# Chunks in pairs on TensorE in an RWKV-5 attention with a SoLU feed-forward block

## The chip, the cores and the metric

The kernel runs on one core of one Trainium2 chip. The metric is the device time of one execution in microseconds (us), lower is better; where several runs of the same kernel stand together, their median is used.

## What is computed

Two blocks follow one another. The first is the RWKV-5 recurrence with batch 4, 8 heads, 768 steps and head size 48; the second takes its result, 3072 tokens of 384 values, through a feed-forward block of width 1024 with a softmax gate and a normalisation.

```
for t in range(S):
    cur = einsum('bhd,bhe->bhde', u * k_t, v_t)
    y[:, :, t] = einsum('bhd,bhde->bhe', r_t, state + cur)
    state = w * state + einsum('bhd,bhe->bhde', k_t, v_t)
x = y.transpose(0, 2, 1, 3).reshape(B * S, H * D)
h = x @ w_in
solu = h * softmax(h)
ln = (solu - mean(solu)) / sqrt(var(solu) + 1e-6) * g_ln
out = ln @ w_out
```

Inputs and results are float32. The weights `w_in`, `w_out` and `g_ln` come as 64-bit floats or as words of that layout, and the kernel converts them itself.

## The kernel before, in words

The kernel is `direct_path`. It assumes that the decays `w` and the weights lie in sane ranges, computes everything on that assumption, and at the end forms one flag, `bad`; if it is set, a slow path (`general_path`, L19) does the work over. With these inputs the flag isn't set.

**Chunks.** The sequence of each batch is cut into 6 chunks of 128 steps. With 4 batches these are N = 24 units (L458), ordered so that the four batches of one chunk follow one another. All work is done per unit, and a unit's state is needed again only four units later.

**What a unit needs.** `load` (L465) fetches k, r and v. `decay_k` and `decay_r` (L671, L678) multiply k and r by powers of the decay on GpSimd; `weigh` (L685) forms r times k times u there, and `sum_own` (L690) sums it per head on VectorE. `diagonal` (L694) writes these sums into the diagonal of the score tile AT, eight ScalarE instructions. k and r are needed turned (channels on the partitions). Up to unit 8, `turn_r` and `turn_k` (L706, L713) do it with TensorE transposes into PSUM and an evacuation. From unit 9 (`FIRST`) on, `halve_rk` (L853) splits the 32-bit words into 16-bit halves on ScalarE (k) and VectorE (r), a transposing DMA on SP's queue turns them (`turn`, L831), and `join_rk` (L863) puts them together again on VectorE. `scores` (L726) multiplies turned k by turned r, 16 matmuls in tiles of 64 by 64, into the PSUM tile `pss` of two banks, and copies what lies above the diagonal into AT with one masked copy (L735). `finish` (L749) computes y, first the product with the state, 12 matmuls in four column tiles of 32, then AT times v, 16 matmuls, and copies it to `xT` on ScalarE (L772). Then it forms k times v for the state (`kv_ps`, L778), adds it to the state on VectorE (L784) and multiplies by the decay on GpSimd (L785).

**The feed-forward part.** `ffn_in` (L790) multiplies xT by w_in: 6 matmuls of 512 columns into two PSUM banks (`h_ps`), and an exponential on ScalarE with its sum (L798). `unit` (L801) makes solu on VectorE (L805, L807) and then centres and squares it on ScalarE (L809, L810). `deviation` (L813) forms the scale on GpSimd. `halve_ln`, the transposing DMA and `join_ln` (L842, L848) turn solu like r and k. `ffn_out` (L867) multiplies by w_out, 8 matmuls of 384 columns, scales the result on ScalarE (L879) and stores it. A float32 matmul shows as two records in the trace, so 6 matmuls are x12.

**Order.** The schedule is written by hand: the order of the calls in the loop at L887 is the order of the instructions on each engine, and each engine works its queue in that order. At step i, the loop does scores of unit i+1, finish of i, `ffn_in` and `unit` of j = i-2 (LA = 2) and `ffn_out` of l = i-7 (LO = 5 more). From i = 7 on, one step is on TensorE: h, o, scores, y, kv. Until i = 6 there is no `ffn_out` and the weights are converted in between.

**Buffers.** [...] `psA` holds `pss` (2 banks), `psH` the h tile (2 banks), and `psM` rotates four banks among everything else (turned r and k, tables, y, kv, o). In SBUF, `halves` and the raw weight words share a ring of six (L505, L825), `kp` has 4 buffers, `e` 2, `lnT` 2.

**Checks.** `check_range` (L636) fetches the decays once more as a row at step 10 and compares them, on one partition. From step 12 on, `load_weights` fetches the 14 weight pieces (6 of w_in with 512 columns, 8 of w_out with 384) once more, one a step, and `check_words` (L555) takes their absolute sum on ScalarE and their minimum on VectorE. `check_sums` (L646) puts everything together at the end.

Of the kernel before, what the change touches and what calls it, by code (L numbers as in the profile page):

```python
# [399 lines left out]
def direct_path(  # L400
# [50 lines left out]
    psM = ctx.enter_context(tc.tile_pool(name="psM", bufs=4, space=PSUM))  # L451
# [27 lines left out]
    wrow = const.tile([1, dm], F32, name="wrow")  # L479
# [8 lines left out]
    pss = psA.tile([128, 2, HP, T], F32, name="at")  # L488
    nc.vector.memset(pss, 0.0)
# [13 lines left out]
    def load_weights(j):  # L503
        dst, src, _ = pieces[j]
        raws[j] = wpool.tile([128, dst.shape[1], 2], U32, tag="raw", name="raw", bufs=6)  # L505
        nc.sync.dma_start(out=raws[j].rearrange("p n o -> p (n o)"), in_=src)
# [48 lines left out]
    def check_words(j):  # L555
        raw = raws.pop(j)
        mag = wpool.tile([128, raw.shape[1]], F32, tag="mag", name="mag", bufs=2)
        nc.scalar.activation(out=mag, in_=raw[:, :, 1].bitcast(F32), func=ACT.Abs,
                             accum_out=total[:, j : j + 1])
        nc.vector.tensor_reduce(out=least[:, j : j + 1], in_=mag, axis=AX.X, op=ALU.min)  # L560
# [26 lines left out]
    for St in states:  # L587
# [12 lines left out]
                            op0=ALU.max, op1=ALU.min)  # L600
    for j in range(8):
        if j < 7:
            nc.vector.tensor_mul(pw[:, 0, j + 1], pw[:, 0, j], pw[:, 0, j])
            nc.vector.reciprocal(out=pw[:, 1, j], in_=pw[:, 0, j])
        if j == 0:
            nc.vector.tensor_copy(out=fore[:, :, T - 1 : T], in_=pw[:, 1, 0].unsqueeze(2))
        else:
            n = 1 << (j - 1)
            nc.vector.tensor_mul(tab[:, :, :, T - 2 * n : T - n], tab[:, :, :, T - n : T],
                                 pw[:, :, j - 1].unsqueeze(3).to_broadcast([128, 2, HP, n]))  # L610
# [6 lines left out]
    def turn_table(table, out):  # L617
        ps = psM.tile([128, HP, 128], F32, tag="m", name="kd_ps")
        for a in range(HP):
            nc.tensor.transpose(ps[:, a, :], table[:, a, :], ident)  # L620
        nc.scalar.copy(out=out, in_=ps)  # L621
# [11 lines left out]
    all_ok = const.tile([1, 1], F32, name="all_ok")  # L633
    bad = flag.tile([1, 1], mybir.dt.int32, name="bad")

    def check_range():  # L636
        nc.sync.dma_start(out=wrow, in_=w.rearrange("h d -> (h d)").partition_broadcast(1))

        ok = small.tile([1, dm], F32, tag="ok", name="ok", bufs=1)
        ok2 = small.tile([1, dm], F32, tag="ok2", name="ok2", bufs=1)  # L640
        nc.vector.tensor_single_scalar(out=ok, in_=wrow, scalar=LOW, op=ALU.is_ge)
        nc.vector.tensor_single_scalar(out=ok2, in_=wrow, scalar=HIGH, op=ALU.is_le)
        nc.vector.tensor_mul(ok, ok, ok2)
        nc.vector.tensor_reduce(out=all_ok, in_=ok, axis=AX.X, op=ALU.min)

    def check_sums():  # L646

        L = len(pieces)
        good = small.tile([128, 2, N + L], F32, name="good", bufs=1)
        low = small.tile([128, 1], F32, name="low", bufs=1)  # L650
        nc.vector.tensor_single_scalar(out=good[:, 0, :N], in_=sums, scalar=1.0 / MOST,
                                       op=ALU.is_ge)
        nc.vector.tensor_single_scalar(out=good[:, 1, :N], in_=sums, scalar=MOST, op=ALU.is_le)
        nc.vector.tensor_single_scalar(out=good[:, 0, N:], in_=least, scalar=FLOOR, op=ALU.is_ge)
        nc.vector.tensor_single_scalar(out=good[:, 1, N:], in_=total, scalar=CEIL, op=ALU.is_le)
        nc.vector.tensor_reduce(out=low, in_=good, axis=AX.XY, op=ALU.min)
        n_ps = psM.tile([1, 1], F32, tag="m", name="n_ps")
        nc.tensor.matmul(n_ps, low, ones, start=True, stop=True)
        nc.vector.tensor_scalar(out=bad, in0=n_ps, scalar1=all_ok, scalar2=127.5,
                                op0=ALU.mult, op1=ALU.is_lt)  # L660
# [10 lines left out]
    def decay_k(i):  # L671
        X = live.setdefault(i, {})
        X["kp"] = apool.tile([128, H, P], F32, name="kp", bufs=4)
        nc.gpsimd.tensor_mul(X["kp"].rearrange("p h d -> p (h d)"),  # L674
                             kpads[i % NLD].rearrange("p h d -> p (h d)"),
                             kdec.rearrange("p a d -> p (a d)"))
# [29 lines left out]
    def turn_r(i):  # L706
        rT = factors(i)["rT"]
        ps = psM.tile([128, HP, T], F32, tag="m", name="tr_ps")
        for a in range(HP):
            nc.tensor.transpose(ps[:, a, :], pair(rpads[i % NLD], a), ident)  # L710
        nc.vector.tensor_mul(rT, ps, fore)

    def turn_k(i):  # L713
        X = live[i]
        ps = psM.tile([128, HP, T], F32, tag="m", name="tk_ps")

        for a in range(HP):
            nc.tensor.transpose(ps[:, a, :], pair(X["kp"] if i > 0 else kpads[0], a), ident)  # L718
        if i > 0:
            nc.scalar.copy(out=X["kT"], in_=ps)  # L720
        else:
            nc.vector.tensor_mul(X["kT"], ps, back)
# [3 lines left out]
    def scores(i):  # L726
        X = live[i]
        A4 = X["AT"].rearrange("p (a q) t -> p q a t", q=2)
        for a in range(HP):
            for c in range(2):  # L730
                for q in range(2):
                    rows = slice(q * P, q * P + D)
                    nc.tensor.matmul(pss[ts(c, P), q, a, c * P :], X["kT"][rows, a, ts(c, P)],  # L733
                                     X["rT"][rows, a, c * P :], start=True, stop=True)
        nc.vector.copy_predicated(A4, later.unsqueeze(1).to_broadcast([128, 2, HP, T]), pss)  # L735
# [13 lines left out]
    def finish(i):  # L749
# [19 lines left out]
        for n, (m, h, at) in enumerate(inner):  # L769
            into(m, vf[:, at : at + 32], AT[:, h, :], last[m] == n)  # L770
        X["xT"] = fpool.tile([128, KD, 128], F32, name="xT", bufs=LA + 1)
        nc.scalar.copy(out=X["xT"], in_=y_ps)  # L772
        if c < C - 1:
            kv_ps = psM.tile([128, HP, D], F32, tag="m", name="kv_ps")
            for a in range(HP):
                for g in range(4):
                    h = 2 * a + g // 2
                    nc.tensor.matmul(kv_ps[ts(g, 32), a], X["kp"][:, h, ts(g % 2, 32)],  # L778
                                     vt[:, h, 0:D], start=True, stop=True)
            for q in range(2):  # L780
                wT = pw[ts(q, P), 0, 7].unsqueeze(2).to_broadcast([P, HP, D])
                S = St[ts(q, P), :, q]
                if c > 0:
                    nc.vector.tensor_add(S, kv_ps[ts(q, P)], S)  # L784
                    nc.gpsimd.tensor_mul(S, S, wT)  # L785
                else:
                    nc.vector.tensor_mul(S, kv_ps[ts(q, P)], wT)


    def ffn_in(i):  # L790
# [6 lines left out]
        e = X["e"] = fpool.tile([128, dff], F32, name="e")  # L797
# [89 lines left out]
    for i in range(-2, N + LA + LO):  # L887
        j, l = i - LA, i - LA - LO
        early = l < 0
        if i == -1:  # L890
            nc.sync.dma_start(out=g_sb, in_=moe_g_ln.rearrange("(c p) -> p c", p=128))
        if 0 <= i and i + 5 < N:
            load(i + 5, "kr")
        if 0 <= i and i + 3 < N:
            load(i + 3, "v")
        early_h = l <= 0
        if early_h and i >= LA:
            ffn_in(j)
# [4 lines left out]
        if i == -2:  # L903
            turn_r(0)
            turn_k(0)
            turn_table(back, kdec)
# [8 lines left out]
        if -2 < i and i + 2 < N:  # L915
            if i + 2 < FIRST:
                turn_r(i + 2)
            elif not early_h:
                join_rk(i + 2)
            if early_h and i >= LA:  # L920
                unit(j)
            if early_h and i + 2 >= FIRST:
                join_rk(i + 2)
            if i < 0 or i >= LA:
                sum_own(i + 2)
            if i + 2 < FIRST:
                turn_k(i + 2)
# [5 lines left out]
        if i + 3 < N and i != 1:  # L933
# [10 lines left out]
        if 1 <= i and i + 3 < N:  # L944
            weigh(i + 3, nc.gpsimd)
        if 0 <= j - 1 < N:
            deviation(j - 1)
        if i == 10:
            check_range()
        if 12 <= i < 12 + len(pieces):  # L950
            load_weights(i - 12)
        if 13 <= i < 13 + len(pieces):
            check_words(i - 13)
        if 0 <= l + 2 < N:
            halve_ln(l + 2)
        if 0 <= l + 1 < N:
            join_ln(l + 1)
        if i + 3 < N:
            halve_rk(i + 3)
        if not early:  # L960
            if j < N and not early_h:
                ffn_in(j)
            if i + 2 < N:
                diagonal(i + 2)
            if j < N and not early_h:
                unit(j)
            if l == N - 1:
                check_sums()
            ffn_out(l)
        if 0 <= i + 1 < N:  # L970
            scores(i + 1)
        if i < 0:
            diagonal(i + 2)
        if 0 <= i < N:
            finish(i)
        if i == 1:
            turn_table(fore, rdec)
            sum_own(3)
        if early and 0 <= i:
# [3 lines left out]
        if i >= LA:  # L983
            for p in before:
                convert_d(p)
            for p in now:
                convert_b(p)
    return bad
# [42 lines left out]
```

## Time and profile before

| | us |
|---|---|
| median of 3 runs | 354.89 |
| the three runs | 355.28, 354.89, 354.89 |
| the profiled execution, its own time | 355.35 |
| its span from the first to the last instruction | 353.5 |
| TensorE matmul busy | 338.0 |
| ScalarE busy | 242.1 |
| VectorE busy | 210.8 |
| GpSimd busy | 176.5 |
| granted TensorE clock (mean) | 0.997 |

The span is what the profile can see; what is left of the profiled execution's time lies around it. PE is TensorE, ACT ScalarE, DVE VectorE, POOL GpSimd, SP the queue from which most DMAs are issued. In a timeline each line has a start, a length (both us), the engine, the line of the kernel, the operation, the tile written and those read, the shape and a count. Neighbouring like instructions are put into one line, and lines may overlap because the engines are pipelined. A bracket at the end gives the idle time before the line and what ended it.

### The profile page before, as it was taken

What the parts mean: (1) busy time and instruction counts of PE and PEld (TensorE: products, weight loads), DVE (VectorE), ACT (ScalarE), POOL (GpSimd) and SP (SyncE); (2) the same over time, 40 slices, a digit from 0 to 9 for tenths busy, and PEclk for the clock granted to TensorE, in tenths of its full rate; (3) what the DMA queues carried; (4) which work ended last, traced back from release to release, by engine and by line L of the source; (5) the groups of instructions that cost most, each with busy time, mean ns of one, the idle gap of its engine ahead of it and who ended that gap; (6) DMA issues with size and microseconds to landing.
All of it is one profiled execution on the core that took longest, in us unless ns stands there. A gap on an engine that the chain in (4) does not pass through costs nothing.

```text
span 353.5 us, 8407 instructions
## 1 busy us (share of the span) xinstructions
PE 338.0 (96%) x3427; PEld 204.8 (58%) x3427; DVE 210.8 (60%) x323; ACT 242.1 (68%) x457; POOL 176.5 (50%) x196
## 2 busy tenths in 40 slices
PE   2699999999999999999999999999999999999993
PEld 2485566656566556566566566565565565555563
DVE  7795888886468567665865765765771441323220
ACT  3765988988897667677867778778687464465510
POOL 3879667784865754945945846746730000000000
PEclk9999999999999999999999999999999999999998
DMA  7998997259999868988997979857663523551641
GB/s 164 266 237 183 252 209 126 51 105 162 189 186 163 150 122 154 195 174 185 188 159 174 206 146 184 187 130 146 150 129 62 126 69 59 128 126 47 139 105 33
DMA packets 164878, 52.75 MB, mean 149 GB/s; under 512 B 157917, under 2 KB 161246, under 8 KB 164830
## 3 DMA queue, kind: packets, MB, share of 16 engines
q1 hardware_dynamic: 164686, 51.92, 71.9%
q8 instruction: 29, 0.48, 0.6%
q10 hardware_dynamic: 144, 0.20, 0.2%
q14 instruction: 19, 0.16, 0.2%
HBM read 26.94 MB, written 4.72 MB: 90 GB/s over the span
## 4 chain that ended last, share of the span: by engine, by line
PE 90%; issue 3%; POOL 2%; DVE 2%; ACT 1%; DMA 1%; POOLq 0%; DVEq 0%
PE o_ps L877 35%; PE h_ps L795 35%; PE y_ps L760 10%; PE at L733 6%; PE kv_ps L778 2%; PE tk_ps L718 1%; PE tr_ps L710 1%; POOL kp L674 1%; DMA wq<-in_w_dram 1%; ACT AT L698 1%; POOL rku L687 1%; DVE part L530 0%; DVE ma L532 0%; POOL w_in_sb L540 0%; DVE solu L807 0%
## 5 line engine op out<-in xcount | busy, mean ns | idle before, releaser
L795 PE MATMUL h_ps<-w_in_sb,xT 128*128 128x512 f32 x288 | 129.8, 600 | 0.7 <-DVE solu L807 0.5
L877 PE MATMUL o_ps<-w_out_sb,lnT 128*128 128x384 f32 (+1 forms) x400 | 127.3, 473 | 0.0
L877 PEld LDWEIGHTS o_ps<-w_out_sb,lnT 128*128 128x128 f32 x400 | 75.1, 190 | 52.8 <-issue 9.1
L795 PEld LDWEIGHTS h_ps<-w_in_sb,xT 128*128 128x128 f32 x288 | 52.8, 190 | 60.7 <-issue 58.1
L698 ACT ACTIVATE AT<-ident,own 128x128 f32<-128x128 f32 x192 | 58.6, 391 | 6.2 <-DVE own L692 6.2
L785 POOL TENSOR_TENSOR state<-state,pw 64x192 f32<-64x192 f32 x32 | 25.6, 800 | 63.2 <-DVE state L784 62.0
L735 DVE COPY_PREDICATED AT<-later,at 128x1024 f32<-128x1024 uint32 x24 | 31.9, 1329 | 31.4 <-PE at L733 31.4
L845 ACT COPY halves<-solu 128x2048 uint16<-128x2048 uint16 x24 | 45.4, 1893 | 0.0
L839 DVE COPY lnT<-halves 128x2048 uint16<-128x2048 uint16 x24 | 37.4, 1559 | 11.7 <-DMA halves<-halves 11.7
L809 ACT ACTIVATE solu<-solu,st 128x1024 f32<-128x1024 f32 x24 | 27.5, 1148 | 22.6 <-DVE solu L807 22.6
L798 ACT ACTIVATE e<-h_ps 128x1024 f32<-128x1024 f32 x24 | 24.5, 1021 | 18.3 <-PE h_ps L795 18.3
L816 POOL TENSOR_SCALAR st<-st 128x1 f32<-128x1 f32 x24 | 7.0, 292 | 59.2 <-ACT e L810 59.2
L674 POOL TENSOR_TENSOR kp<-kpad,kdec 128x512 f32<-128x512 f32 x24 | 31.6, 1317 | 7.6 <-ACT kdec L621 6.5
L807 DVE SCALAR_TENSOR_TENSOR solu<-h_ps,st,e 128x1024 f32<-128x1024 f32 x24 | 30.8, 1284 | 2.5 <-DVE st L805 0.5
L688 POOL TENSOR_TENSOR rku<-rku,rpad 128x384 f32<-128x384 f32 x23 | 28.9, 1256 | 1.8
L839 DVE COPY rk<-halves 128x2048 uint16<-128x2048 uint16 x15 | 21.7, 1444 | 11.4 <-DMA halves<-halves 11.0
L733 PE MATMUL at<-rk 48*64 48x128 f32 (+1 forms) x768 | 27.9, 265 | 0.0
L733 PEld LDWEIGHTS at<-rk 48*64 48x64 f32 x768 | 21.8, 139 | 10.4 <-issue 8.8
L681 POOL TENSOR_TENSOR rp<-rpad,rdec 128x512 f32<-128x512 f32 x15 | 27.4, 1829 | 0.0
L860 DVE COPY halves<-rp 128x1024 uint16<-128x1024 uint16 x15 | 19.8, 1319 | 11.3 <-POOL rp L681 11.3
L760 PE MATMUL y_ps<-AT,vt 128*32 128x128 f32 x768 | 26.3, 279 | 0.0
L810 ACT ACTIVATE e<-solu 128x1024 f32<-128x1024 f32 x24 | 25.4, 1057 | 0.8
(82 smaller groups left out, 320.3 us busy)
## 6 DMA issues: line engine op xcount, KB each, us to landing
raw<-in_moe_w_in_dram SPq DMA_DIRECT2D x12, 512.0 KB, 5.7
raw<-in_moe_w_out_dram SPq DMA_DIRECT2D x16, 384.0 KB, 4.7
kpad<-in_k_dram SPq DMA_DIRECT2D x24, 192.0 KB, 4.2
rpad<-in_r_dram SPq DMA_DIRECT2D x24, 192.0 KB, 4.6
vt<-in_v_dram SPq DMA_DIRECT2D x24, 192.0 KB, 4.5
out_dram<-o SPq DMA_DIRECT2D x23, 192.0 KB, 2.2
halves<-halves SPq DMA_TRANSPOSE x39, 4.6
u_bc<-in_u_dram ACTq DMA_DIRECT2D x1, 192.0 KB, 3.8
```

The costliest lines, as they stand in the source:

```text
L674: nc.gpsimd.tensor_mul(X["kp"].rearrange("p h d -> p (h d)"), kpads[i % NLD].rearrange("p h d -> p (h d)"), kdec.rearrange("p a d -> p (a ...
L688: engine.tensor_mul(rku, rku, rpads[i % NLD][:, :, 0:D])
L698: nc.scalar.activation(out=AT[:, h, :], in_=ident, func=ACT.Copy, scale=X["own"][:, h])
L733: nc.tensor.matmul(pss[ts(c, P), q, a, c * P :], X["kT"][rows, a, ts(c, P)], X["rT"][rows, a, c * P :], start=True, stop=True)
L735: nc.vector.copy_predicated(A4, later.unsqueeze(1).to_broadcast([128, 2, HP, T]), pss)
L760: nc.tensor.matmul(y_ps[32 * g : 32 * g + 32, j, :], lhsT, rhs, start=(g not in opened), stop=stop, skip_group_check=True)
L795: nc.tensor.matmul(h_ps[:, ts(n, NX)], X["xT"][:, j, :], w_in_sb[:, j, ts(n, NX)], start=(j == 0), stop=(j == KD - 1))
L807: nc.vector.scalar_tensor_tensor(out=solu, in0=X["h"], scalar=rs, in1=X["e"], op0=ALU.mult, op1=ALU.mult, accum_out=tot)
L809: nc.scalar.activation(out=solu, in_=solu, func=ACT.Identity, scale=-float(dff), bias=tot)
L839: nc.vector.tensor_copy(out=words.bitcast(U16).rearrange("p n (t o) -> p o n t", o=2), in_=turned)
L845: nc.scalar.copy(out=both.rearrange("p (o n) -> p o n", o=2), in_=split(X["solu"]))
L877: nc.tensor.matmul(o_ps, X["lnT"][:, f, :], w_out_sb[:, f, part], start=(f == 0), stop=(f == KF - 1))
```

## The change

Seven edits belong together.

1. From i = 7 on the loop goes in steps of two. One round does: sum_own and join_rk of units i+1 and i+2; decays and weigh of i+3 and i+4; then two halves, each with halve_ln, join_ln, ffn_in, unit, halve_rk, check_words and ffn_out of one unit; then the scores of i+1 and i+2, their masked copies, y of i and i+1, kv of both and the state of both.
2. `scores` is split: the matmuls stay in it, and `take_scores` does the masked copy, now one for each of the two banks. Scores of even units go to one pair of banks and those of odd units to another. `finish` is split into `heads` (y), `take_y` (its copy), `outer` (kv of one or two units in one PSUM tile) and `update` (the state).
3. The PSUM tile `pss` becomes four banks; `psM` goes from four buffers to two. `turn_r` and the second table use bank 2, `turn_k` bank 3.
4. `check_range` and its row are gone. The decays are copied out of PSUM in the prologue and compared in `check_sums`, in two instructions on 128 partitions.
5. The words for the check get a ring of their own with one buffer; the ring of the halves is theirs alone. `mag` goes from two buffers to one.
6. `kp` goes from 4 buffers to 5, `e` from 2 to 1.
7. The one-by-one loop runs only up to i = 6.

```diff
-    psM = ctx.enter_context(tc.tile_pool(name="psM", bufs=4, space=PSUM))
+    psM = ctx.enter_context(tc.tile_pool(name="psM", bufs=2, space=PSUM))
...
-    pss = psA.tile([128, 2, HP, T], F32, name="at")
-    nc.vector.memset(pss, 0.0)
+    pss = [psA.tile([128, HP, T], F32, name=f"at{n}") for n in range(4)]
+    for ps in pss[:2]:
+        nc.vector.memset(ps, 0.0)
...
-    def load_weights(j):
+    def load_weights(j, tag="raw", bufs=6):
         dst, src, _ = pieces[j]
-        raws[j] = wpool.tile([128, dst.shape[1], 2], U32, tag="raw", name="raw", bufs=6)
+        raws[j] = wpool.tile([128, dst.shape[1], 2], U32, tag=tag, name="raw", bufs=bufs)
...
+    nc.vector.tensor_copy(out=decays, in_=wd_ps)
...
+        nc.vector.tensor_single_scalar(out=good[:, 0, N + L :], in_=decays, scalar=LOW,
+                                       op=ALU.is_ge)
+        nc.vector.tensor_single_scalar(out=good[:, 1, N + L :], in_=decays, scalar=HIGH,
+                                       op=ALU.is_le)
...
-        n_ps = psM.tile([1, 1], F32, tag="m", name="n_ps")
+        n_ps = psH.tile([128, dff], F32, tag="h", name="n_ps")[0:1, 0:1]
...
     def scores(i):
         X = live[i]
-        A4 = X["AT"].rearrange("p (a q) t -> p q a t", q=2)
+        ps = pss[2:] if i > LA + LO and i % 2 else pss[:2]
...
-        nc.vector.copy_predicated(A4, later.unsqueeze(1).to_broadcast([128, 2, HP, T]), pss)
+        X["scores"] = ps
+
+    def take_scores(i):
+        A4 = live[i]["AT"].rearrange("p (a q) t -> p a q t", q=2)
+        for q in range(2):
+            nc.vector.copy_predicated(A4[:, :, q, :], later.to_broadcast([128, HP, T]),
+                                      live[i]["scores"][q])
...
+    def outer(chunks):
+        chunks = [i for i in chunks if i < N and units[i][1] < C - 1]
+        if not chunks:
+            return
+        kv_ps = psM.tile([128, 2, HP, D], F32, tag="m", name="kv_ps")
+        for n, i in enumerate(chunks):
...
+    for i in range(LA + LO, N + LA + LO, 2):
+        j, l = i - LA, i - LA - LO
+        for n in (i, i + 1):
+            if n + 5 < N:
+                load(n + 5, "kr")
+            if n + 3 < N:
+                load(n + 3, "v")
+        new = [n for n in (i + 1, i + 2) if FIRST <= n < N]
+        for n in new:
+            sum_own(n)
+        late = i == LA + LO
+        if late:
+            ffn_in(j)
+            unit(j)
+        for n in new:
+            join_rk(n)
+        for n in (i + 3, i + 4):
+            if n < N:
+                decay_k(n)
+                decay_r(n)
+                weigh(n, nc.gpsimd)
+        for n in (j - 2, j - 1):
+            if LO - 1 <= n < N:
+                deviation(n)
+        for half in range(2):
+            if l + half + 2 < N:
+                halve_ln(l + half + 2)
+            if half == 0 and new:
+                diagonal(new[0])
+            if l + half + 1 < N:
+                join_ln(l + half + 1)
+            if j + half < N and not (late and half == 0):
+                ffn_in(j + half)
+                unit(j + half)
+            if i + half + 3 < N:
+                halve_rk(i + half + 3)
+            if half == 0 and len(new) > 1:
+                diagonal(new[1])
+            for p in checked:
+                check_words(p)
+            checked = [checks.pop(0)] if checks and i > LA + LO else []
+            for p in checked:
+                load_weights(p, "check", 1)
+            if l + half == N - 1:
+                check_sums()
+            ffn_out(l + half)
+        now = [n for n in (i + 1, i + 2) if n < N]
+        for n in now:
+            scores(n)
+        for n in now:
+            take_scores(n)
+        now = [n for n in (i, i + 1) if n < N]
+        for n in now:
+            heads(n)
+            take_y(n)
+        outer(now)
+        for n in now:
+            update(n)
```

## The prediction

> **What bounds the kernel now.** I read the page first: busy times, then the chain that ended last.
>
> ```profile
> PE 338.0 (96%) x3427; PEld 204.8 (58%) x3427; DVE 210.8 (60%) x323; ACT 242.1 (68%) x457; POOL 176.5 (50%) x196
> ...
> PE 90%; issue 3%; POOL 2%; DVE 2%; ACT 1%; DMA 1%; POOLq 0%; DVEq 0%
> ```
>
> TensorE is the bound, and a gain must come out of its own time. So I read its timeline for one chunk of the steady loop (start, length, instruction; the lengths overlap, so I take start to next start):
>
> ```profile
> 208.51 5.42 PE L795 MATMUL h_ps<-w_in_sb,xT 128*128 128x512 f32 x12
> 213.76 5.32 PE L877 MATMUL o_ps<-w_out_sb,lnT 128*128 128x384 f32 x16
> 219.02 1.09 PE L733 MATMUL at<-rk 48*64 48x128 f32 x32
> 220.04 0.86 PE L760 MATMUL y_ps<-rk,state 128*32 128x128 f32 x24
> 220.72 1.06 PE L760 MATMUL y_ps<-AT,vt 128*32 128x128 f32 x32
> 221.59 0.52 PE L778 MATMUL kv_ps<-vt,kp 128*32 128x48 f32 x32
> 222.04 5.42 PE L795 MATMUL h_ps<-w_in_sb,xT 128*128 128x512 f32 x12
> ```
>
> Start to start: h 5.25, o 5.26, scores (at) 1.02, y 0.68 + 0.87, kv 0.45; 13.53 us a chunk, 27.07 for two, with no bracket of idle time. Near the end, where h and o follow one another:
>
> ```profile
> 300.87 5.42 PE L795 MATMUL h_ps<-w_in_sb,xT 128*128 128x512 f32 x12
> 306.12 5.32 PE L877 MATMUL o_ps<-w_out_sb,lnT 128*128 128x384 f32 x16
> 311.28 5.31 PE L795 MATMUL h_ps<-w_in_sb,xT 128*128 128x512 f32 x12
> 316.43 7.90 PE L877 MATMUL o_ps<-w_out_sb,lnT 128*128 128x384 f32 x24
> ```
>
> Here o takes 5.16 and the second h 5.15: each change of tile shape costs about 0.10. Next, who follows TensorE closest: ScalarE, in the same loop.
>
> ```profile
> 186.90 1.02 ACT L798 ACTIVATE e<-h_ps 128x1024 f32<-128x1024 f32 x1 [0.45 <-PE h_ps L795]
> 187.82 0.19 ACT L798 ACTIVATION_READ_ACCUMULATOR e<-h_ps 128x1 f32 x1
> 187.91 2.43 ACT L698 ACTIVATE AT<-ident,own 128x128 f32<-128x128 f32 x8
> 190.67 1.15 ACT L809 ACTIVATE solu<-solu,st 128x1024 f32<-128x1024 f32 x1 [0.32 <-DVE solu L807]
> 191.85 1.06 ACT L810 ACTIVATE e<-solu 128x1024 f32<-128x1024 f32 x1
> ```
>
> ScalarE works about 10.2 of each 13.5 us. The diagonal (L698) stands between e and solu and fills the time in which VectorE makes solu. Last, VectorE and GpSimd side by side:
>
> ```profile
> 72.93 1.34 DVE L839 COPY lnT<-halves 128x2048 uint16<-128x2048 uint16 x1
> 74.17 1.48 DVE L860 COPY halves<-rp 128x1024 uint16<-128x1024 uint16 x1
> ```
>
> ```profile
> 73.16 1.94 POOL L688 TENSOR_TENSOR rku<-rku,rpad 128x384 f32<-128x384 f32 x1
> ```
>
> L688 takes 1.00 alone and L860 0.68; GpSimd waited until the first copy ended, ran 0.83, and the second copy, though queued at once behind the first, waited for it.
>
> **What the Trainium skill says.** "TensorEngine Tiling (Array Packing)", Key Properties: changing the tiling mode drains the TensorE; the trace agrees, at 0.10 us a change. "SBUF — State Buffer", Who interferes with whom: a VectorE copy in a two-port mode and a GpSimd instruction lock each other out for a whole instruction, and who issues first has it; the lines above agree. "TensorE: Matmul & The Clock Gate", Part 1, on engine queue depths: ScalarE and VectorE are strict FIFO; the trace shows nothing out of program order on them.
>
> **The gain.** For two chunks TensorE now does h, o, h, o, at, at, y, y, kv. One change each goes at o to at (5.26 - 5.16 = 0.10), at to y (0.10, as the others), kv to h (y goes to h in 0.99 without kv, 0.87 before kv: about 0.11) and in the first h (5.25 - 5.15 = 0.10); y after y saves 0.03, the excess of the first state product. Sum 0.43: 26.64 us a pair. Pairs with two y: i = 7, 9, ... 21, eight: **-3.44 us**.
>
> **What it puts on the path.** I walk one pair, time 0 at its first h. TensorE without waits: h to 5.25, o(l) 10.41, h 15.56, o(l+1) 20.82, at 21.75, at 22.77, y(i) 24.32, state part of y(i+1) 24.98, its AT part 25.85, kv 26.64. Two things can hold it. y(i+1) takes the PSUM buffer of o(l+1) (psM falls from 4 to 2), so ScalarE must have copied o(l+1) out. And its AT part needs take_scores(i+1), now in the same round instead of one earlier; both stand at the end of their queues, behind check_words.
>
> VectorE first. update waits for kv: four adds (L784, pitch 0.38, first at 0.14) end at 1.64; two sum_own (0.45 apart) let the joins begin at 2.58. GpSimd follows the adds by 0.43: four products of 0.50, the last until 2.80, then kp and rp (1.27 each alone). So three copies of the two-port kind (join_rk twice, join_ln) now stand back to back, and GpSimd's decay work begins at the same moment. Before, only one copy and one of kp/rp met, with 2.5 us of idle VectorE behind. A copy needs 1.18 after the lock is free (L839 lnT at 184.64 to 186.56 with kp until 185.37), a product 1.09 (rp 185.33 to 187.65). Taking turns: join_rk 2.80-3.98, kp -5.08, join_rk -6.26, rp -7.35, join_ln -8.53. The reciprocal (L805) starts at 8.45 instead of 6.60, when the exponential's sum is there (5.45 + 1.11 + 0.03): **late by 1.86**.
>
> ScalarE by start to start: e 1.01, then its solu waits for VectorE: e to solu is 2.72 with VectorE free (2.65 at 34.00, 2.74 near the end). solu 1.18, square 1.06, kp halves 0.95, diagonal 2.34, check 0.66 (w_in piece) or 0.55 (w_out), o 0.46, halve_ln 1.80. From e(j) at 5.45: 2.72 + 1.86 + 1.18 + 1.06 + 0.95 + 2.34 + 0.66 + 0.46 + 1.80 = 13.03, so e(j+1) at 18.49; its h ended at 15.56, so ScalarE is late here. Then 2.72 + 1.18 + 1.06 + 0.95 = 5.91: check at 24.40, o(l+1) copied by 25.63; y(i+1) starts 1.4 late. The check's sum ends at 25.17, VectorE's minimum (L560) frees it at 25.79, and then come the two masked copies of take_scores. A copy of 512 columns isn't in the trace: the whole one takes 1.33, half of that is 0.67, and two VectorE passes of 512 columns from PSUM take 0.69; I take 0.75 with pitch 0.67 (0.67 to 0.90 for the ends). AT is ready at 27.20 and its part starts at 27.26 instead of 24.98: **2.29 a pair with w_in pieces**. Behind the waiting matmul stand kv and the next h, so the exponential, the state adds and the next pair's clock move with it; nothing of it is made up.
>
> Per pair: i = 9 has no check in its first half: 1.63. i = 11 and 13: 2.29 each. i = 15 (one piece of each kind): 2.05. i = 17 and 19: 1.94 each. i = 7 has no check and its single join_rk behind unit: the walk has o(1) copied at 24.23 against 24.32, none. i = 21 has no decay work left, so no lock and no kp halves: none. Sum **+12.14 us**. Without the lock, taking 1.86 off, they would be 0.43, 0.43, 0.19, 0.08 and 0.08: 1.2.
>
> **The edits that I cost at nothing, and why.** check_range goes: four VectorE passes of 2.0 us and a DMA, at i = 10, where TensorE shows no idle. Two compares more at the end (0.17 each) lie in some 1.5 us in which VectorE waits for n_ps; n_ps takes an h bank free since h(23). The decays copy (0.16) and the split memset (0.91 in one, about 1.0 in two, an estimate) lie in the prologue, where VectorE waits 0.24 for wd_ps and 0.92 for tr_ps; the split masked copy costs 0.1 twice on busy VectorE there, and its next wait of 0.29 (L711 at 24.04) takes it: I book +0.1, between 0 and 0.5. turn_r and turn_k with a bank each: the evacuations (L711 24.04-24.73) are over before the next use (L620 at 26.79). SP's queue: per pair six loads (about 7 us of issue), four transposes (mean 3.0), two checks (1.2 or less), two outputs (0.36): 23 of 27 us. The new check loads wait for ScalarE's last check; behind them wait the output and the next transposes, and both wait for later ScalarE work anyway. The one with least room, rk's second transpose, is issued near 24.5 and landed in 4.3 to 7.8 before; join_rk wants it at 5.1 of the next pair, 9 us later.
>
> **Sum.** Profiled execution 355.35 (span 353.5): 355.35 - 3.44 + 12.14 + 0.1 = 364.15. The median shown is 0.46 lower, 354.89, so I forecast **363.7**, slower by 2.5%.
>
> **Rivals.**
> - Faster. VectorE's three copies keep the shared port and GpSimd waits them out; the place is L805 at 6.6 us of a pair. Stalls 1.2: 354.89 - 3.44 + 1.2 + 0.1 = **352.8**. It decides if the joins end by 6.6. For it: a copy queued behind a copy might never release. Against: at 74.17 and twice more (108.39, 134.61) GpSimd got in between.
> - In between: only one GpSimd product gets in. Late by about 0.75, stalls 0.5, 1.2, 1.2, 0.9, 0.8, 0.8 = 5.4: **357.0**.
> - Much slower: six loads in a bunch make the transposes late. DMA engines are 65 to 100% busy in the stretches of this loop; if join_rk waits 1 us in six pairs more: **370**.
>
> **Chances.** Forecast 0.58 (own range 360 to 367), faster 0.17, in between 0.15, much slower 0.10. Range 353 to 367.5: it leaves out half of the fast case and the slow one. About 0.2% (0.7 us) is what a measurement of this kernel can tell from no change. Faster 0.17, same 0.05 (the edge between fast and in between), slower 0.78.
>
> **What the profile would show.** Right: brackets of idle TensorE at y and its AT part, released by ScalarE's o and VectorE's masked copy, some 2 us in each pair from i = 9 to 19 and none at 7 and 21; join_rk and kp stretched to over 2 us in turns; second o's and h's of 5.15. Wrong: joins of 1.3 us in a row; TensorE at 26.6 us a pair; or waits of join_rk on DMA.

## The result and the profile after

The changed kernel takes **368.81 us** (median of 4 runs, 367.84 to 369.04) against 354.90 for the kernel before: 1.0384 times as long, 95% interval 1.0364 to 1.0404. Its profiled execution took 369.04 us, its span 367.0; 355.35 and 353.5 before. The forecast was 363.7 with a range up to 367.5, so the sign was right and the time lies above the range.

The same two lines of the page as before, busy time by engine and the chain that ended last:

```profile
PE 339.3 (92%) x3427; PEld 205.7 (56%) x3427; DVE 210.9 (57%) x347; ACT 240.8 (66%) x457; POOL 178.5 (49%) x196
...
PE 33%; DVE 27%; ACT 24%; issue 10%; DMA 3%; POOL 1%; SPq 0%; DVEq 0%; ACTq 0%; POOLq 0%
```

No engine has noticeably more to do, and the busy shares look like those of a kernel bound by TensorE. The chain says otherwise: TensorE's share of it fell from 90% to 33%, and VectorE and ScalarE have the rest. The chain now goes back and forth between the engines.

TensorE's timeline of one pair, the round i = 11:

```profile
133.29 5.42 PE L814 MATMUL h_ps<-w_in_sb,xT 128*128 128x512 f32 x12
138.55 5.33 PE L896 MATMUL o_ps<-w_out_sb,lnT 128*128 128x384 f32 x16
143.71 5.31 PE L814 MATMUL h_ps<-w_in_sb,xT 128*128 128x512 f32 x12
148.86 5.33 PE L896 MATMUL o_ps<-w_out_sb,lnT 128*128 128x384 f32 x16
154.11 1.96 PE L728 MATMUL at<-rk 48*64 48x128 f32 x64
156.01 0.86 PE L761 MATMUL y_ps<-rk,state 128*32 128x128 f32 x24
156.69 1.06 PE L761 MATMUL y_ps<-AT,vt 128*32 128x128 f32 x32
158.97 0.86 PE L761 MATMUL y_ps<-rk,state 128*32 128x128 f32 x24 [1.23 <-ACT o L898]
159.78 0.41 PE L761 MATMUL y_ps<-AT,vt 128*32 128x128 f32 x4
160.39 0.96 PE L761 MATMUL y_ps<-AT,vt 128*32 128x128 f32 x26 [0.19 <-DVE AT L735]
```

h to o is 5.26 as before, but o to h and h to o within the pair are 5.16 and 5.15. The saving is there. It is lost in the last three lines: y of the second chunk waits first for ScalarE's copy of o, then for the masked copy. To see where each pair stands, take the time from the first h of a round to the first h of the next:

| round i | 7 | 9 | 11 | 13 | 15 | 17 | 19 | 21 | 23 | sum |
|---|---|---|---|---|---|---|---|---|---|---|
| before, two chunks | 27.19 | 27.04 | 27.07 | 27.07 | 27.07 | 27.07 | 26.73 | 26.39 | 22.59 | 238.22 |
| predicted | 26.76 | 28.24 | 28.93 | 28.93 | 28.69 | 28.58 | 28.24 | 25.96 | 22.59 | 246.92 |
| after | **31.84** | 28.51 | 28.77 | 28.77 | 28.53 | 28.41 | 28.07 | 25.91 | 23.15 | 251.96 |

These rounds became 13.74 us longer, what lies ahead of them and behind them 0.13 and 0.16 shorter; together that is the span's 13.5. Against the forecast two entries stand out: round 7, 5.08 more, and round 23, 0.56 more. All others are within 0.3.

**The steady rounds.** VectorE and GpSimd at the head of round 11, which starts at 133.29:

```profile
134.96 1.01 DVE L687 TENSOR_REDUCE own<-rku 128x8 f32<-128x384 f32 x2
135.89 3.65 DVE L858 COPY rk<-halves 128x2048 uint16<-128x2048 uint16 x2
139.44 2.38 DVE L858 COPY lnT<-halves 128x2048 uint16<-128x2048 uint16 x1
141.71 0.14 DVE L824 RECIPROCAL st<-sums 128x1 f32<-128x1 f32 x1
...
158.39 0.69 DVE L562 TENSOR_REDUCE least<-mag 128x1 f32<-128x512 f32 x1 [3.38 <-ACT mag L560]
158.99 2.59 DVE L735 COPY_PREDICATED AT<-later,at 128x512 f32<-128x512 uint32 x4
```

```profile
136.15 2.21 POOL L669 TENSOR_TENSOR kp<-kpad,kdec 128x512 f32<-128x512 f32 x1
138.32 2.31 POOL L676 TENSOR_TENSOR rp<-rpad,rdec 128x512 f32<-128x512 f32 x1
140.60 2.05 POOL L682 TENSOR_TENSOR rku<-kpad,u_bc 128x384 f32<-128x384 f32 x1
```

The three copies of VectorE stretch to 3.65 (two) and 2.38 (one), where one alone takes about 1.3; GpSimd's products stretch to 2.21, 2.31 and 2.05 where 1.27, 1.27 and 1.00 are their times alone. None of these lines has a bracket: each queue is full, and the time is in the instructions. The reciprocal starts 8.42 us into the round.

**Round 7.** TensorE, VectorE and ScalarE:

```profile
96.74 1.06 PE L761 MATMUL y_ps<-AT,vt 128*32 128x128 f32 x32
101.07 1.51 PE L761 MATMUL y_ps<-rk,state 128*32 128x128 f32 x24 [3.27 <-ACT o L898]
102.35 1.82 PE L761 MATMUL y_ps<-AT,vt 128*32 128x128 f32 x32
104.00 0.85 PE L791 MATMUL kv_ps<-vt,kp 128*32 128x48 f32 x64
```

```profile
94.47 1.33 DVE L858 COPY lnT<-halves 128x2048 uint16<-128x2048 uint16 x1 [4.51 <-DMA halves<-halves]
95.69 0.15 DVE L824 RECIPROCAL st<-sums 128x1 f32<-128x1 f32 x1
95.95 1.28 DVE L826 SCALAR_TENSOR_TENSOR solu<-h_ps,st,e 128x1024 f32<-128x1024 f32 x1
```

```profile
78.34 2.44 ACT L693 ACTIVATE AT<-ident,own 128x128 f32<-128x128 f32 x8
80.69 1.00 ACT L817 ACTIVATE e<-h_ps 128x1024 f32<-128x1024 f32 x1
...
97.27 1.15 ACT L828 ACTIVATE solu<-solu,st 128x1024 f32<-128x1024 f32 x1 [3.18 <-DVE solu L826]
...
100.45 0.57 ACT L898 ACTIVATE o<-o_ps,st 128x384 f32<-128x384 f32 x1
```

Read them from the last line back. y(8) takes the PSUM buffer of o(1), whose copy starts at 100.45 and ends at 101.02; that copy stands behind solu of unit 6 on ScalarE, which waited 3.18 for VectorE; and VectorE's solu stands behind join_ln(2), which waited 4.51 for its transposing DMA. That DMA was issued at 87.67, as soon as ScalarE had split the values (85.65 to 87.53), and ScalarE was late from the start: h(5) had ended at about 78.4, but e(5) starts at 80.69, behind the diagonal of the one-by-one loop. On top, y(8) ran slowly: its two parts take 1.28 and 1.65 from start to start, where 0.66 and 0.87 are usual. The windows of TensorE before, in and after it (length, busy time of each engine, granted clock, DMA share, GB/s) show why:

```profile
72.94:101.00 28.06, 24.72 (x184) 13.67 (x176) 18.82 (x25) 23.16 (x40) 16.26 (x16) 0.99 0.96 153
101.00:104.78 3.78, 3.71 (x120) 3.38 (x120) 0.00 (x0) 0.92 (x4) 0.00 (x0) 0.61 1.01 113
104.78:133.30 28.52, 27.43 (x305) 16.07 (x297) 17.22 (x23) 19.47 (x37) 16.83 (x16) 1.00 0.81 156
...
100.51:103.93 3.42, 2.86 (x56) 2.59 (x60) 0.00 (x0) 0.88 (x3) 0.00 (x0) 0.50 0.94 87
```

The granted clock, TensorE's share of its full speed, is the third number from the end. It is 0.61 over the 3.8 us behind the idle time and full before and after; the last line, a narrower window, shows 0.50 for 3.42 us. So the wait of 3.27 us cost about 1.4 us more. It need not do so in every execution: the three that took 368.80 to 369.04 us have a mean clock of 0.995, while the fourth, with 367.84, has 1.000, which leaves no room for such a stretch.

### The profile page after: what moved, and what is told of

It reads as the page before. It is cut to its first block, busy times and chain, and to the rows that moved or that the text cites. A ratio compares the mean times of both kernels' runs of the same rounds, so it can differ in the third digit from the quotient of the medians.

```text
span 367.0 us, 8468 instructions
## 1 busy us (share of the span) xinstructions
PE 339.3 (92%) x3427; PEld 205.7 (56%) x3427; DVE 210.9 (57%) x347; ACT 240.8 (66%) x457; POOL 178.5 (49%) x196
## 4 chain that ended last, share of the span: by engine, by line
PE 33%; DVE 27%; ACT 24%; issue 10%; DMA 3%; POOL 1%; SPq 0%; DVEq 0%; ACTq 0%; POOLq 0%
PE o_ps L896 14%; PE h_ps L814 12%; DVE solu L826 6%; DVE rk L858 6%; ACT AT L693 6%; ACT solu L828 5%; PE y_ps L761 4%; DVE lnT L858 4%; ACT halves L864 4%; DVE AT L735 3%; ACT e L817 3%; DVE state L803 2%; ACT halves L878 2%; DVE own L687 2%; DMA halves<-halves 2%
## 5 line engine op out<-in xcount | busy, mean ns | idle before, releaser
L804 POOL TENSOR_TENSOR state<-state,pw 64x192 f32<-64x192 f32 x32 | 16.2, 505 | 86.8 <-DVE state L803 85.0
L669 POOL TENSOR_TENSOR kp<-kpad,kdec 128x512 f32<-128x512 f32 x24 | 39.0, 1625 | 7.1 <-ACT kdec L623 6.6
L562 DVE TENSOR_REDUCE least<-mag 128x1 f32<-128x384 f32 (+1 forms) x14 | 8.5, 610 | 57.4 <-ACT mag L560 57.4
L835 POOL TENSOR_SCALAR st<-st 128x1 f32<-128x1 f32 x24 | 9.6, 398 | 49.2 <-ACT e L829 49.1
L735 DVE COPY_PREDICATED AT<-later,at 128x512 f32<-128x512 uint32 x48 | 31.5, 727 | 0.0
L761 PE MATMUL y_ps<-AT,vt 128*32 128x128 f32 x768 | 29.5, 285 | 1.1 <-DVE AT L735 1.1
L682 POOL TENSOR_TENSOR rku<-kpad,u_bc 128x384 f32<-128x384 f32 x23 | 30.5, 1325 | 0.0
L858 DVE COPY rk<-halves 128x2048 uint16<-128x2048 uint16 x15 | 26.7, 1829 | 0.9 <-DMA halves<-halves 0.9
L777 ACT COPY xT<-y_ps 128x384 f32<-128x384 f32 x24 | 11.4, 474 | 23.7 <-PE y_ps L761 23.7
L761 PE MATMUL y_ps<-rk,state 128*32 128x128 f32 x480 | 17.9, 283 | 9.7 <-ACT o L898 9.7
```

The costliest lines, as they stand in the source:

```text
L682: engine.tensor_mul(rku, kpads[i % NLD][:, :, 0:D], u_bc)
L735: nc.vector.copy_predicated(A4[:, :, q, :], later.to_broadcast([128, HP, T]), live[i]["scores"][q])
L761: nc.tensor.matmul(y_ps[32 * g : 32 * g + 32, j, :], lhsT, rhs, start=(g not in opened), stop=stop, skip_group_check=True)
L858: nc.vector.tensor_copy(out=words.bitcast(U16).rearrange("p n (t o) -> p o n t", o=2), in_=turned)
```

## The experiments

The theory from here on: in rounds 9 to 19 VectorE's joins and GpSimd's products take turns, ScalarE's chain becomes late by it, and `check_words` puts VectorE's part of that lateness ahead of the masked copies; in round 7 `join_ln` holds up `unit`. Times of rounds are read as in the table; their sum over the rounds 9 to 19 is 162.05 before and 171.06 after. All are compared with the kernel before on the same chip. Unless said otherwise, an edit is made on the changed kernel.

**Without the decays (e1).** Takes GpSimd out of the meeting.

```diff
     def decay_k(i):
+        if i >= 12:
+            X["kp"] = kept["kp"]
+            return
```

and the same for `rp` and `rku`; `kept` holds unit 11's tiles.

> From unit 12 on GpSimd's decay products (kp, rp, rku) are left out and unit 11's are used again, so the output is not the reference's. Theory 1 (the shared port: VectorE's three joins and GpSimd's decay work take turns at the start of a round, and solu of the first half comes 1.8 us late): the joins last 1.3 us each, the reciprocal starts about 6.6 us into the round instead of 8.4, rounds i = 9 to 19 fall from 28.0-28.8 us to about 26.7-27.0, about 358. Theory 2 (the work itself is too much for ScalarE and VectorE in a round, GpSimd has nothing to do with it): 368 to 369, rounds unchanged. Round i = 7 stays near 31.8 in both.

Measured: 359.45 us, ratio 1.0126 (1.0109 to 1.0143). VectorE in round 11, which starts at 132.01 here:

```profile
134.60 2.58 DVE L871 COPY rk<-halves 128x2048 uint16<-128x2048 uint16 x2
137.08 1.31 DVE L871 COPY lnT<-halves 128x2048 uint16<-128x2048 uint16 x1
138.67 0.16 DVE L837 RECIPROCAL st<-sums 128x1 f32<-128x1 f32 x1 [0.28 <-ACT e L830]
```

The same copies, queued in the same order, take about 1.3 each, where in the changed kernel the first takes 1.38 and the two behind it 2.38 each, and the reciprocal comes at 6.66 with a bracket: it waits for the exponential, no longer for VectorE. Rounds 9 to 19 sum to 161.85: 9.2 us of the stall go with GpSimd's products. Rounds 11 to 15 take 27.06 to 27.08, where the forecast had a stall of 0.43 without the lock and so 27.07. Round 7 (31.72) lies ahead of unit 12's first use and is nearly as in after.

**Without the words (e2).** Takes the check out of both engines' queues; two constant fills stand for its sums. The second fetch of the weights goes with it, so there is less DMA traffic too; this run alone does not tell the two apart.

```diff
-            for p in checked:
-                check_words(p)
-            checked = [checks.pop(0)] if checks and i > LA + LO else []
-            for p in checked:
-                load_weights(p, "check", 1)
```

> The second fetch of the weights and check_words are left out (constants stand in for their results). Theory 1 (the stall is a chain: late solu, check on ScalarE, minimum on VectorE, masked copies, AT part of y): without the check the masked copies are done before TensorE asks, o(l+1) is copied out at about 24.2 us of the round against 24.3, so rounds i = 9 to 19 take about 26.6 and the whole 357.4. Theory 2 (the two PSUM buffers hold y whatever VectorE does): ScalarE is only 1.3 us earlier per round, the rounds fall by no more than that less what is left, about 361 to 362.

Measured: 358.34 us, ratio 1.0100 (1.0080 to 1.0119); rounds 11 to 19 are 26.74, 26.74, 26.75, 26.74 and 26.40, sum 160.47 with round 9; round 7 is 31.86. The decays still meet the joins, yet 10.6 us go. Neither cause alone makes the stall: the products make ScalarE late, and `check_words` passes that lateness on to TensorE.

**The check last (e3).** Two ways lead from the check to TensorE: ScalarE's part is ahead of the copy of o, whose PSUM buffer y needs; VectorE's minimum is ahead of the masked copies. With the block moved behind `ffn_out(l + half)`, the first is gone and the second later.

```diff
-            for p in checked:
-                check_words(p)
...
             ffn_out(l + half)
+            for p in checked:
+                check_words(p)
```

> check_words and its load move behind ffn_out in each half; nothing is left out. Theory 1 (VectorE's masked copy is the wait that ends last): o is copied out 0.66 us earlier, but the minimum and so the masked copies come about 0.46 later, rounds i = 11 to 19 grow by 0.4 to 0.5, 371 to 371.6. Theory 2 (the copy of o, that is psM with two buffers, is the wait that ends last): rounds shrink by up to 0.66, 365 to 366.

Measured: 372.36 us, ratio 1.0486 (1.0458 to 1.0513). That is above the expected 371.6 because of round 7, which has no check: there the clock stayed at 0.50 for 6.82 us behind the wait, and the round took 32.56 instead of 31.84. TensorE in round 11:

```profile
159.20 0.86 PE L761 MATMUL y_ps<-rk,state 128*32 128x128 f32 x24 [0.58 <-ACT o L898]
161.12 0.41 PE L761 MATMUL y_ps<-AT,vt 128*32 128x128 f32 x4 [1.05 <-DVE AT L735]
161.72 0.96 PE L761 MATMUL y_ps<-AT,vt 128*32 128x128 f32 x26 [0.19 <-DVE AT L735]
```

The wait for o shrank from 1.23 to 0.58, that for the masked copy grew, and the rounds 9 to 19 became longer by 0.45 each. So the masked copy is the wait that ends last, although the profile gives o the larger bracket. A bracket tells when a wait ended, not what would remain without it.

**unit first (e4).** Lets VectorE make solu before the third copy.

```diff
-            if l + half + 1 < N:
-                join_ln(l + half + 1)
             if j + half < N and not (late and half == 0):
                 ffn_in(j + half)
                 unit(j + half)
+            if l + half + 1 < N:
+                join_ln(l + half + 1)
```

> join_ln moves behind ffn_in and unit in each half; nothing is left out. Theory 1: in the first half solu is not behind the third join any more, the reciprocal starts at about 6.6 us, rounds i = 9 to 19 fall by about 1.8 each (10.7 together); in round i = 7 the second solu does not wait for the transposing DMA, 1.8 less, and TensorE's idle stretch is short enough that its clock stays, 1.4 less: about 355. Theory 2 (ScalarE is simply full): solu earlier changes nothing that lasts, no more than 2 us gained, 367.

Measured: 356.90 us, ratio 1.0047 (1.0030 to 1.0064); rounds 9 to 19 sum to 161.80. VectorE in round 11 (from 130.18):

```profile
132.78 3.65 DVE L858 COPY rk<-halves 128x2048 uint16<-128x2048 uint16 x2
136.84 0.16 DVE L824 RECIPROCAL st<-sums 128x1 f32<-128x1 f32 x1 [0.42 <-ACT e L817]
137.11 1.28 DVE L826 SCALAR_TENSOR_TENSOR solu<-h_ps,st,e 128x1024 f32<-128x1024 f32 x1
...
138.32 1.35 DVE L858 COPY lnT<-halves 128x2048 uint16<-128x2048 uint16 x1
```

join_rk still takes 3.65 for two, so the locking is unchanged; but the reciprocal is at 6.66 into the round. The loss was not the slower copies as such but what stood behind them. The 1.9 us that are left against before lie outside the steady rounds: round 7 is 28.93, 1.7 more than before.

**The move in round 7 only (e5).** As e4, but with `if late` ahead of the new place.

> Only in the first paired round (i = 7) join_ln moves behind ffn_in and unit. Theory 1 (there the second solu stands behind a join that waits for a transposing DMA, and ScalarE enters the round 2.3 us late with work of the one-by-one loop): 1.8 us less idle TensorE and no drop of its clock behind it (1.4), so that round falls from 31.8 to about 28.6-28.9, the others stay, 365.8. Theory 2 (ScalarE's backlog alone sets the round): unchanged, 368.8.

Measured: 365.69 us, ratio 1.0304 (1.0288 to 1.0320); round 7 is 28.93, all others within 0.34 of after.

```profile
99.51 0.86 PE L761 MATMUL y_ps<-rk,state 128*32 128x128 f32 x24 [1.73 <-ACT o L898]
100.19 1.06 PE L761 MATMUL y_ps<-AT,vt 128*32 128x128 f32 x32
```

Moving one call in one round gives 2.9 us: 1.5 of the wait, and the slow clock behind it. After 1.73 us of idle time y runs at its usual 0.68 and 0.87.

**The other way: the diagonal into ScalarE's wait (e6).** ScalarE waits for solu in each round (3.36 us in round 11 of after), while the diagonal stands behind it.

```diff
+                if half == 0 and len(new) > 1:
+                    diagonal(new[1])
                 unit(j + half)
...
-            if half == 0 and len(new) > 1:
-                diagonal(new[1])
```

> Only the second diagonal of a round moves, from behind halve_rk to between the exponential and unit of the first half, where ScalarE waits for VectorE. Theory 1 (a chain through ScalarE with a late solu): the 2.3 us of the diagonal vanish in the wait, late solu or not; o(l+1) and the check come 2.3 earlier, rounds i = 9 to 19 about 26.7, round i = 7 unchanged at 31.8, about 358. Theory 2 (the shared port as such costs TensorE time, not its place on ScalarE's chain): rounds stay near 28.5, 368.

Measured: 359.81 us, ratio 1.0124 (1.0101 to 1.0146); rounds 11 and 13 take 26.59, 9 to 19 sum to 161.52. TensorE in round 11, from h at 134.00:

```profile
154.82 1.96 PE L728 MATMUL at<-rk 48*64 48x128 f32 x64
156.72 0.86 PE L761 MATMUL y_ps<-rk,state 128*32 128x128 f32 x24
...
158.27 0.84 PE L761 MATMUL y_ps<-rk,state 128*32 128x128 f32 x24
...
160.59 1.98 PE L814 MATMUL h_ps<-w_in_sb,xT 128*128 128x512 f32 x4
```

No bracket: 26.59 us for a pair, where the forecast's sum gives 26.64 and the kernel before takes 27.07. The whole is above the expected 358 for two reasons outside these rounds: in round 7 the clock was at 0.50 for 6.82 us and the round took 32.64, and rounds 9 and 15 (28.46 and 27.05) have a gap in kv, of which more below. The edit leaves the joins and products as they are; it gives ScalarE back 2.4 us, more than the 1.86 that they cost.

**Both (e7).** e4 and e6 together, to see what limits then.

> join_ln behind unit in every half, and the second diagonal in ScalarE's wait. Theory 1: rounds i = 9 to 19 at the matmuls' own 26.64 to 26.75 (160.3 together), round i = 7 at 28.9, rounds 21 and 23 unchanged: about 355.0. If the gains of the two simply added up (a theory without a bound by TensorE): 368.8 - 11.9 - 10.8 = 346.

Measured: 356.73 us, ratio 1.0054 (1.0039 to 1.0070); sum of 9 to 19 161.48. The pairs stay at 26.59 and go no lower: the bound is now TensorE's own matmuls. Rounds 7 (28.94), 9 (27.56) and 15 (27.90) do not reach it.

**The gaps (e8, e10).** e8 takes e7, puts the diagonal of round 7 into ScalarE's wait too, and in round 25, which has the last h, moves `ffn_out(18)` ahead of `ffn_in(23)` (the lines show only the new places), to cover the 0.6 us in which h(23) waits for y.

```diff
+            if j == N - 1 and half == 0:
+                ffn_out(l)
             if j + half < N and not (late and half == 0):
                 ffn_in(j + half)
+                if new and half == (len(new) == 1):
+                    diagonal(new[-1])
                 unit(j + half)
```

> As the kernel with both, and also: the diagonal of unit 9 goes into ScalarE's wait in the second half of round i = 7, and in round i = 25 ffn_out(18) comes ahead of ffn_in(23), so that h(23) does not wait for y(23) to be copied. Theory 1: round 7 falls from 28.9 to about 27.1 and round 23 from 23.15 to about 22.5; with 160.3 for 9 to 19 that is 2.3 us less than the kernel before in these rounds, about 352.6, faster than before. If the pairing brings TensorE nothing (its saved changes of tile shape are not real): no better than before, 355 or more.

Measured: 360.39 us, ratio 1.0154 (1.0140 to 1.0168): a miss. Round 7 is mended (27.20), but the end lost more. The waits of TensorE from 70 to 330 us (total, times, longest):

```profile
PE o_ps L896 <- DVE lnT L858: 4.3, 1, 4.3
PE kv_ps L791 <- issue: 1.7, 2, 1.0
```

The o that follows h(23) now needs a `join_ln` that stands behind `unit(23)` on VectorE. On top, the clock granted behind this wait was 0.50 for 3.41 us (325.65 to 329.06). e10 is e8 with that one `join_ln` ahead of the unit.

```diff
                 ffn_in(j + half)
+                if j == N - 1:
+                    join_ln(l + 1)
```

> As the kernel with the gaps filled, but in round i = 25 join_ln(19) stays ahead of unit(23): there it stood behind the solu of h(23), and o(19) waited 4.3 us for it. Then round 23 (up to the start of h(23), which now includes o(18)) should fall from 27.75 to about 22.5 + 5.2 = 27.7 and what follows h(23) from 43.05 to about 37.3, together 5 less: 360.4 - 5 = 355; with round 7 at 27.2 and 9 to 19 at 161.4 (two of them 1 us longer at kv than the others) it ends 0.5 to 2 us below the kernel before, 353 to 354.4. If the saved changes of tile shape are eaten by something else in the rest of the kernel: 355 or more.

Measured: 358.31 us, ratio 1.0083 (1.0059 to 1.0106): a second miss. The 4.3 us are gone, but o(21) waits 2.6 for its turned values, since their halves stand behind the exponential of the last unit on ScalarE. Again a slow stretch follows, here in the window from 333.88:

```profile
333.88:337.29 3.41, 3.41 (x6) 1.72 (x6) 1.31 (x1) 0.00 (x0) 0.00 (x0) 0.50 1.09 227
```

Half speed for 3.41 us loses some 1.7 us, an estimate from these two numbers. From h(23) to the end is 41.44 us, with four whole o and the last one in two parts, where 37.3 was expected; the wait and the slow clock together account for the difference. The o's that come after h(23) cover the last unit's chain; using one up ahead of it takes that cover away.

**y ahead (e11).** e4's order, the diagonals as in e8, `ffn_in(23)` in its old place, and in round 23 y(23) ahead of `ffn_out(17)`.

```diff
+            if i == N - 1 and half == 1:
+                heads(i)
+                take_y(i)
             ffn_out(l + half)
...
-        now = [n for n in (i, i + 1) if n < N]
+        now = [n for n in (i, i + 1) if n < N - 1]
```

> join_ln behind unit, the second diagonal (in round 7 the only one) in ScalarE's wait, ffn_in(23) left in its old place, and in round i = 23 y(23) computed ahead of ffn_out(17), so that its copy lies under that. Theory 1: rounds 27.2, 161.4 for 9 to 19, 25.9 and 22.5, the end as in the kernel before: 1.2 us less than before, 353.7. If what is saved on changes of tile shape is not real or goes elsewhere: 355.

Measured: **354.01 us** (10 runs, 353.83 to 354.67), ratio 0.9977 (0.9968 to 0.9987) against 354.83: better than both kernels, by a quarter of a per cent over the one before. Rounds 7 to 23: 27.19, 27.53, 26.59, 26.59, 27.90, 26.59, 26.25, 25.90, 22.59; sum 237.13. The only wait of TensorE left from 70 to 330 us:

```profile
PE kv_ps L791 <- issue: 1.8, 2, 1.1
```

**The decays' check alone (e9).** The kernel before with edit 4 alone.

> The kernel before with edit 4 alone: check_range and its fetch go, the decays are copied out of PSUM in the prologue and compared at the end. By the prediction these cost nothing: 354.9, within 0.5 of the kernel before. If the four VectorE passes or the fetch in the middle were on the path, up to 2 us less, 353; if the copy in the prologue is, up to 0.3 more.

Measured: 354.81 us (22 runs), ratio 0.9995 (0.9985 to 1.0006), each round as before: it costs and gives nothing.

## Why the prediction was right and where it failed

**The gain.** "Sum 0.43: 26.64 us a pair" holds: 26.59, a gain of 0.48, in e6, e7 and e11, once nothing waits.

**The stall in the steady rounds.** The mechanism and the size hold. The reciprocal was put at 8.45 into the round and came at 8.42, the second exponential at 18.49 and came at 18.41, the check at 24.40 and came at 24.32; in round 11 the rest of the AT part was put at 27.26 and came at 27.10. The masked copy of 512 columns, which the trace before did not have, was taken at 0.75 and takes 0.727. The six rounds sum to 171.61 in the forecast and 171.06 on the chip. e1, e2, e4 and e6 each remove one link, and these rounds get 9.2 to 10.6 us shorter; e3 confirms which of the two waits ends last. What the Trainium skill, "SBUF — State Buffer", Who interferes with whom, says of two-port copies and GpSimd locking each other out for a whole instruction agrees, and the run shows what it means when both queues are full: they alternate, for three copies and three products.

**The step that failed: "i = 7 has no check and its single join_rk behind unit: the walk has o(1) copied at 24.23 against 24.32, none".** o(1) was copied out at 28.08 us of the round (101.02), not at 24.23, and the round took 5.08 us more than forecast: 3.27 of waiting, 1.4 of slow clock and 0.4 at its first o. Four things were missing from the step, all seen in round 7's trace:

- The walk started ScalarE's clock at the end of h(5). ScalarE enters the round with work of the one-by-one loop, and e(5) starts 2.3 us after its h. A margin of 0.09 us is not "none".
- The walk had `join_ln` as a copy that takes VectorE's time, and asked of DMAs only whether `join_rk` would wait. `join_ln(2)` waited 4.51 us for its DMA, with `unit(6)` behind it in VectorE's queue. e5 moves that one call and gets 2.9 us back; with the diagonal moved into ScalarE's wait as well (e8, e11) round 7 is 27.2.
- A wait of 3.27 us was followed by a granted clock of 0.50 for 3.42 us, which no step allowed for: 1.4 us of the 5.1.
- The forecast looked at the smaller psM only for y(i+1). Here the first o of the round takes the buffer of y(6) and starts just behind its copy on ScalarE (77.97 to 78.45): o(0) starts 5.56 us after h(5) instead of 5.25, and h(6) 5.27 after o(0) instead of 5.16. That stays in e11, where round 7 takes 27.19, as before the change: the forecast gain of 0.43 does not appear in this round.

How the wait divides between ScalarE's late start and the DMA was not separated, since the one delays the other. Round 7 alone is about as large as the whole miss (369.04 against 364.15 in the profiled execution); that the smaller differences, 0.55 less in rounds 9 to 19, 0.56 more in round 23 and some tenths ahead and behind, nearly cancel is luck.

**Round 23, "22.59" unchanged.** The mis-sized term is one bracket: h(23) waits 0.60 for the copy of y(23), because nothing lies between that y and it. The round took 0.56 more; e11 puts y(23) earlier and has 22.59 again.

**The edits at nothing.** e9 shows it for edit 4. The other edits of this list weren't tried alone. The prologue was booked at +0.1 and became 0.13 shorter, which says nothing either way: up to the first h of round 7 the changed kernel and the runs made from it take between 72.45 and 73.97.

**The rivals.** Faster, with VectorE's copies keeping the port, fails on the reciprocal at 8.42; in between fails too, since GpSimd got in between every two copies. Much slower by late transposes is right in kind for one place: `join_rk` waits for DMAs 0.9 us in the whole execution, but `join_ln` in round 7 was held by one. The forecast had asked that question of `join_rk` alone.

**Where the gain went.** In e11 the rounds 11, 13, 17, 19 and 21 each gain 0.48, 2.4 in all. Round 7 gains nothing. Rounds 9 and 15 lose 0.49 and 0.83 against before, with a gap in the middle of kv that the profile puts down to "issue" and to no engine. In round 9 of e11:

```profile
126.42 0.67 PE L791 MATMUL kv_ps<-vt,kp 128*32 128x48 f32 x43
127.78 0.45 PE L791 MATMUL kv_ps<-vt,kp 128*32 128x48 f32 x21 [0.68 <-issue]
```

Without it, about 2 us more would be had. It appears in e6, e7, e8, e10 and e11, always in these rounds, and shorter in e4. Its cause wasn't tried and stays open, but the traces hold a pointer: each of these gaps ends 1.3 to 1.6 us after a 16 KB packet of the instruction queue (q8 on the page) has come in, in e11 at 126.36 and 207.43, with TensorE going on at 127.78 and 208.88. A TensorE that waits for its own next instructions would look like this. In the changed kernel the same packet (128.74 to 129.67) falls into the wait for o, and no gap shows.

## What to carry to other kernels

When two steps are merged, write down for each in-order queue what will stand back to back and who waits behind it; here the new burst cost time only because two urgent instructions (solu, masked copy) stood behind it, and moving one call, not removing any work, gave 12 of the 14 us back. Walk the first and the last round of a new loop with the lateness that each engine brings in from the code ahead, and don't book a margin of a tenth of a microsecond as safe. Before moving work ahead at the end of a kernel, ask which chain it was covering.

## What the runs showed of the hardware

- With 3.27 us of idle TensorE came a granted clock of 0.50 for 3.42 us, and y(8) took 1.4 us longer. It was 0.50 for 3.41 us with waits of 4.25 us (e8) and 2.60 us (e10), and for 6.82 us with waits of 3.28 and 3.35 us (e3, e6). The slow stretch began near the end of the wait, from 1.3 us ahead of it (e6) to 0.9 us behind it (e1). With waits of 1.73 us (e4, e5, e7) the clock stayed full. The Trainium skill, "TensorE: Matmul & The Clock Gate", Part 1, tells of half rate after an idle window of about 3.4 us; the traces agree on the half rate, but here 2.60 us of idle time was enough.
- VectorE's copies and GpSimd's products took turns while both had them queued (round 11, three of each): a copy of 1.29 us becomes up to 2.38, a product of 1.27 up to 2.31, without a bracket in the profile.
- kv of two chunks, 64 matmul records in 0.8 us, has 0.2 to 1.4 us of idle time in rounds 9 and 15, in e6, e7, e8, e10 and e11 always after 43 records in round 9 and after 46 in round 15. Each gap follows the end of a 16 KB packet on the instruction queue by 1.3 to 1.6 us; that this is the cause is not shown.
